# Squared-ReLU attention with a routed feed-forward part: the moving operand of four score chunks laid out in token order by eight transfers

## The chip, the core and the metric

One NeuronCore of one Trainium2 chip runs the whole program as a single launch. The metric is the time of one execution in microseconds of device time; three runs of the kernel before are given by their median. One further execution was taken under the hardware profiler, and every row below comes from that one.

The names used here: PE is TensorE's matmul, PEld its weight load, DVE is VectorE, ACT is ScalarE, POOL is GpSimd, SP is SyncE. An added "q" (SPq, PEldq) means the sequencer of that engine, which issues transfers and waits for semaphores.

## The reference

```python
scores = np.matmul(z, z.transpose(0, 2, 1)) / S      # z: (8, 3136, 64)
attn = np.maximum(scores, 0.0) ** 2
x = u * np.matmul(attn, v)                           # u, v: (8, 3136, 256)
...
s = np.einsum('bsd,d->bs', x, w_gate)                # per batch: the 128 tokens with the largest s
h = np.maximum(x[b, top] @ w1, 0.0)                  # w1: (256, 1024), w2: (1024, 256)
out[b, top] = x[b, top] + sigmoid(s[b, top])[:, None] * (h @ w2)
```

All arithmetic is in float32, and the scores of a batch form a symmetric matrix of 3136 by 3136. The second part, the routed one, is small beside the first and is woven into it. This study is about the first line, `z` times `z` transposed.

## The kernel before, in words

**Chunks and tiles.** The 3136 query tokens of a batch are cut into seven chunks: five of 512 columns (numbers 0 to 4), one of 256 and one of 320. The 3136 keys are cut into tiles of 128 and handled two at a time; such a pair of key tiles for one chunk is a *slot*, and the last half tile is a slot of its own. The program is one list of slots (`slots`), batch after batch and chunk after chunk, and the order of every engine is written out from that list by hand (`tc.manual_schedule()`), with scores issued three slots (`LEAD`) ahead of their use.

**Scores.** `scores` (L413) multiplies, for one slot, the key tiles by the moving operand `Z[b, c]`. A float32 value is carried as a high and a low float32r part; `ZH` and `ZL` hold them, and `Z` stacks the high part on partitions 0 to 63 and the low part on partitions 64 to 127, so that two matmuls for one key tile (one with weights from `ZH`, one with weights from `ZL`) make the full product. A slot of two key tiles thus has four score matmuls in a row, which this text calls a *quartet*: ZH, ZL, ZH, ZL. Then ACT and DVE square the result, split it into `hi` and `lo` (L423, L424, L434, L483), and `mix` (L519) multiplies `V` by it into `acc`, twelve matmuls a slot.

**Symmetry.** Since the scores are symmetric, a square that an earlier chunk computed is not computed again: DVE transposes it in blocks of 32 (L452, L471) into `aT`, SP stores it to HBM (`squares`, L458 and L466) and a later chunk fetches it (`qk`, L362), so that its slot is an *old* one, without score matmuls. A chunk of number c below 5 therefore computes scores only for key tiles from 4c on. Its own second pair of tiles (`is_second`) needs only the last 256 of the 512 columns.

**The layout of z.** The block transposes want the keys of a chunk in a mixed order, so `ZH` and `ZL` hold a chunk of 512 tokens as (t f a): f counts its four groups of 128 tokens, t the four quarters of a group and a the 32 tokens of a quarter. A key tile, 128 neighbouring columns, is then one quarter of each of the four groups. The moving operand has to give its columns in token order, (f t a). `bring_z` (L243 to L266) copies the chunk's columns of `ZH` and `ZL` from SBUF to SBUF into the tile `Z` (two buffers) ahead of the chunk, seven slots before its first one. Two ways of doing it are there:

- a chunk of 512 columns is copied as it lies, by two transfers (L258), one for each half of the partitions, and the matmul then reads it through a view that puts the columns into order, in runs of 32 columns:

```python
Z[b, c] = t.rearrange("p (t f a) -> p f t a", t=GT, a=Q) if w == CH else t
```

- the chunks of 256 and 320 columns are put into order by the transfer itself, 128 columns at a time (L263, and L265 for the last 64 columns): four or six transfers, whose source is gathered in runs of 32 columns (128 bytes); the matmul reads 256 or 320 contiguous columns.

The very first chunk of all is written by ACT and DVE instead of by transfers.

**SP's queue.** Nearly all transfers are issued by SP, in the order in which the program lists them: `z` and `v` of the next batch, the squares stored and fetched, `u`, the results. They rotate through eight semaphores (DMAHW0 to DMAHW7), and an issue waits until the transfer that had its semaphore before it has landed.

Of the kernel before, what the change touches and what calls it, by code (L numbers as in the profile page):

```python
# [19 lines left out]
CH = 512  # L20
GT = 4
Q = 32
# [62 lines left out]
def attention_then_routed_ffn(ctx: ExitStack, tc: tile.TileContext, zt, ut, v, wg, w1, w2, cst, cst16, keys, outs, at, cap):  # L85
# [101 lines left out]
    for o in range(0, W, 2 * D):  # L187
        kk, f = divmod(o, F)
# [11 lines left out]
    def by_rows(z, c0, n):  # L200

        g = c0 // CH * CH
        rows = slice((c0 - g) // P, (c0 - g + n) // P)
        return z[:, g : g + CH].rearrange("p (t f a) -> p f t a", t=GT, a=Q)[:, rows]

    Z = {}
# [38 lines left out]
    def bring_z(b, c):  # L245

        c0, w = CHUNKS[c]
        t = const.tile([P, CH], F32R, name="Z", tag="Z", bufs=2)[:, :w]
        for rows, z in ((slice(0, 64), ZH), (slice(64, P), ZL)):
            if b == 0 and c == 0:  # L250
                src, to = (by_rows(x, 0, CH)[rows] for x in (z, t))
                st = staged["z", 0, 0][rows].rearrange("p (f t a) -> p f t a", t=GT, a=Q)
                if z is ZH:
                    nc.scalar.copy(to, st)
                else:
                    nc.vector.tensor_tensor(to, st, by_rows(ZH, 0, CH)[rows].bitcast(F32), op=ALU.subtract)
            elif w == CH:
                nc.sync.dma_start(t[rows].bitcast(F32), z[rows, c0 : c0 + w].bitcast(F32))  # L258
            else:
                for o in range(0, w, P):  # L260
                    if c0 + o < NJ * P:
                        src = by_rows(z, c0 + o, P)[rows, 0]
                        nc.sync.dma_start(t[rows, o : o + P].rearrange("p (t a) -> p t a", a=Q).bitcast(F32), src.bitcast(F32))  # L263
                    else:
                        nc.sync.dma_start(t[rows, o:].bitcast(F32), z[rows, c0 + o : c0 + w].bitcast(F32))  # L265
        Z[b, c] = t.rearrange("p (t f a) -> p f t a", t=GT, a=Q) if w == CH else t  # L266

    def stage_v(b, g, queues=(nc.sync,) * GT):

# [853 lines left out]
    for b in range(B):  # L1123
        k0 = b * per

        for i in range(NCH):
            if b == 0:
                k = (0, 0, 0, 1, 3, 5, 6)[i]
            elif i < WHOLE:
                k = k0 - per + (i + 1) * SLOTS + 7  # L1130
            else:
                k = k0 - 1 + 4 * (i - WHOLE)
            use = lambda b=b, i=i: prep_z(b, i)
            if b:
                at_slots(k, lambda b=b, i=i: stage_z(b, i), use, 0.6, lead=5 if i < WHOLE else 2)
            elif i > 2:
                at_slot(k, lambda i=i: prep_z(0, i, 1 if i < WHOLE else WHOLE), 0.6, 0.7)
                if i == WHOLE:
                    loads.append((2, lambda: stage_z(0, WHOLE, S + 64 - WHOLE * CH)))
                elif 3 < i < WHOLE:  # L1140
                    loads.append((max(1, k - 3), lambda i=i: more_z(0, i, 1)))
        for g in range(NJ // 2 + 1):
            k = k0 - 10 + 3 * g // 2 if b else max(1, g - 2)
            if b or g > 2:
                at_slot(k, lambda b=b, g=g: prep_v(b, g))
            if (b or g > 4) and g % 2 == 0:
                loads.append((k - (3 if b else 2), lambda b=b, g=g: stage_v(b, g // 2)))
        for c in range(NCH):
            if b or c:
                at_slot(k0 + c * SLOTS - LEAD - 4, lambda b=b, c=c: bring_z(b, c))  # L1150
        for c in range(NCH):
            at_slot(k0 + c * SLOTS + 7, lambda b=b, c=c: load_u(b, c))
# [73 lines left out]
    def start():  # L1226
        warm(12)
        stage_z(0, 0)
        first = moe.tile([P, 1], F32, name="g", tag="g", bufs=2)
        nc.scalar.copy(first, idle[0][:, :1])  # L1230
        stage_z(0, 1, (WHOLE - 1) * CH, CH)
        stage_v(0, 0, (nc.scalar, nc.scalar, nc.sync, nc.sync))
        stage_v(0, 1)
        more_z(0, 2, 1)
        more_z(0, 3, 1)
        low_parts = []
        prep_z(0, 0, on=lambda *x, **how: low_parts.append(lambda: nc.vector.tensor_tensor(*x, **how)))
        bring_z(0, 0)
        for fn in low_parts:
            fn()  # L1240
        prep_z(0, 1)
        more_scores(0)
        prep_v(0, 0, nc.vector)
        busy["pool"] = 3.0
        more_scores(1)
        square_scores()
        prep_v(0, 1)
        settle_scores()
        prep_z(0, 2, 1)
        prep_v(0, 2)  # L1250
        warm(2)
        stage_v(0, 2)

    order = ExitStack()
# [131 lines left out]
```

## Time and profile before

| | |
|---|---|
| median of 3 runs | 2118.13 us (2117.64 to 2118.53) |
| the profiled execution | 2115.92 us |
| its span, first to last instruction | 2114.1 us |
| PE busy | 2095.5 us, 99% |
| DVE, POOL, ACT busy | 1520.9, 1345.6, 1221.6 us |
| DMA queue of SP | 430752 packets, 417.89 MB, 72.2% of 16 engines' span |
| transfers under 512 bytes a packet | 148864 packets |
| score matmuls, L413 | 760 with ZH and 760 with ZL |
| acc matmuls, L519 | 8064 in two large groups |
| granted TensorE clock | full in all 40 slices |

The profile lists busy time by engine, then the chain of waits (followed back from the last instruction), then groups of instructions by line, then the transfers. The end of a matmul is modelled, and successive ones overlap, so that the duration of a matmul row is longer than its share of PE's time. What a matmul really takes from PE is read from the timeline instead: the distance from its start to the start of the next one. A timeline row gives the start of its first instruction, the time up to the modelled end of its last one, the engine, the line, output and inputs, and how many equal instructions stand in the row.

### The profile page before, as it was taken

The numbers are of one execution on the slowest core, as the hardware profiler recorded it, in microseconds if no ns is written. First come the engines' busy times: TensorE is split into PE (matmuls) and PEld (weight loads), VectorE is DVE, ScalarE is ACT, GpSimd is POOL, SyncE is SP. The second block draws the span as 40 slices with busy tenths as digits, with TensorE's granted clock in tenths as the row PEclk, the third lists the DMA queues.
The fourth block names the chain that finished last, engine by engine and source line by source line (L and its number), as shares of the span: only waits on it lengthen the run. The fifth ranks groups of instructions, "written<-read, shape, count | busy, mean of one in ns | idle before, by whom it ended". The sixth has DMA issues, their size and how long they took to land.

```text
span 2114.1 us, 31795 instructions
## 1 busy us (share of the span) xinstructions
PE 2095.5 (99%) x10583; PEld 1754.7 (83%) x10583; DVE 1520.9 (72%) x2304; ACT 1221.6 (58%) x1493; POOL 1345.6 (64%) x703
## 2 busy tenths in 40 slices
PE   8999999999999999999999999999999999999998
PEld 6788988889888898888988889888897888887788
DVE  8767678765877667776678766786667776787776
ACT  7564576545765457654676546755466554765543
POOL 6676577655866558765576655866567656666643
PEclk9999999999999999999999999999999999999999
DMA  7798766788667876778767777677776776765862
GB/s 199 202 260 224 216 186 180 186 235 219 185 192 190 232 219 190 193 192 224 217 193 199 191 223 216 187 201 194 207 236 177 206 187 177 210 193 162 221 175 93
DMA packets 431973, 422.28 MB, mean 200 GB/s; under 512 B 148864, under 2 KB 340160, under 8 KB 428224
## 3 DMA queue, kind: packets, MB, share of 16 engines
q1 hardware_dynamic: 430752, 417.89, 72.2%
q0 software_dynamic: 768, 2.10, 0.3%
q8 instruction: 83, 1.36, 0.3%
q14 instruction: 82, 0.67, 0.1%
q10 hardware_dynamic: 288, 0.26, 0.0%
HBM read 235.31 MB, written 172.23 MB: 193 GB/s over the span
## 4 chain that ended last, share of the span: by engine, by line
PE 87%; DMA 3%; DVE 2%; issue 2%; ACT 2%; POOL 2%; SPq 1%; POOLq 0%; DVEq 0%; ACTq 0%
PE acc L519 71%; PE sc L413 14%; POOL lo L483 1%; ACT a L423 1%; ACT hi L424 1%; PE h L1037 1%; DVE a L434 1%; DMA qk<-squares_narrow 1%; PE y L1081 1%; DMA qk<-squares 0%; DMA squares<-aT 0%; DVE lo L483 0%; SPq L381 0%; DVE ut L564 0%; SPq L466 0%
## 5 line engine op out<-in xcount | busy, mean ns | idle before, releaser
L519 PE MATMUL acc<-hi,V 128*128 128x512 f32 (+2 forms) x5376 | 1232.9, 367 | 3.0 <-ACT hi L424 0.8
L483 POOL TENSOR_TENSOR lo<-a,hi 128x1024 fp32r<-128x1024 f32 (+2 forms) x327 | 756.2, 2315 | 609.7 <-DVE a L434 484.3
L519 PEld LDWEIGHTS acc<-hi,V 128*128 128x128 f32 x5376 | 932.9, 188 | 171.2 <-DVE ut L564 8.9
L423 ACT ACTIVATE a<-sc 128x1024 f32<-128x1024 f32 (+4 forms) x408 | 363.3, 890 | 540.9 <-PE sc L413 431.2
L519 PE MATMUL acc<-lo,V 128*128 128x512 f32 (+2 forms) x2688 | 668.7, 365 | 3.2 <-POOL lo L483 3.1
L519 PEld LDWEIGHTS acc<-lo,V 128*128 128x128 f32 x2688 | 474.3, 188 | 86.8 <-POOL lo L483 5.6
L434 DVE TENSOR_TENSOR a<-sc,a 128x1024 f32<-128x1024 f32 (+3 forms) x334 | 338.2, 1012 | 278.3 <-ACT hi L424 257.7
L391 ACT CAST hi<-qk 128x1024 fp32r<-128x1024 f32 (+2 forms) x320 | 275.5, 863 | 245.0 <-PE acc L519 201.5
L452 DVE STREAM_TRANSPOSE aT<-a 128x512 f32<-128x512 f32 (+1 forms) x520 | 341.0, 691 | 84.4 <-ACT a L429 57.3
L424 ACT ACTIVATE hi<-a 128x1024 fp32r<-128x1024 f32 (+4 forms) x408 | 377.4, 925 | 18.1 <-PE acc L519 0.5
L483 DVE TENSOR_TENSOR lo<-qk,hi 128x1024 fp32r<-128x1024 f32 (+2 forms) x223 | 299.5, 1350 | 72.1 <-ACT hi L391 69.6
L413 PE MATMUL sc<-Z,ZH 128*128 128x512 f32 (+2 forms) x760 | 282.0, 375 | 3.4 <-DVE a L434 2.4
L413 PE MATMUL sc<-Z,ZL 128*128 128x512 f32 (+2 forms) x760 | 281.9, 375 | 0.7 <-DVE ZL L120 0.7
L483 POOL TENSOR_TENSOR lo<-qk,hi 128x1024 fp32r<-128x1024 f32 (+2 forms) x97 | 188.8, 1950 | 57.7 <-ACT hi L391 39.1
L413 PEld LDWEIGHTS sc<-Z,ZH 128*128 128x128 f32 x760 | 142.8, 188 | 34.5 <-DVE a L434 6.1
L413 PEld LDWEIGHTS sc<-Z,ZL 128*128 128x128 f32 x760 | 142.7, 188 | 26.4 <-DVE ZL L120 1.1
L120 POOL TENSOR_TENSOR V<-vst,V 128x512 fp32r<-128x512 f32 x89 | 126.4, 1424 | 31.5 <-ACT V L119 27.0
L585 POOL TENSOR_TENSOR ut<-x,w_run 128x1024 f32<-128x1024 f32 (+2 forms) x52 | 127.3, 2449 | 24.4 <-DVE x L576 22.4
L429 ACT ACTIVATE a<-a 128x1024 f32<-128x1024 f32 x74 | 78.5, 1061 | 2.3
L119 ACT CAST V<-vst 128x512 fp32r<-128x512 f32 x95 | 57.8, 608 | 38.3 <-DMA vst<-in_v 38.1
L120 POOL TENSOR_TENSOR ZL<-zst,ZH 128x512 fp32r<-128x512 f32 (+2 forms) x56 | 76.0, 1362 | 2.9 <-ACT ZH L119 2.8
L564 DVE SCALAR_TENSOR_TENSOR ut<-acc,ut 128x512 f32<-128x512 f32 (+2 forms) x112 | 64.0, 612 | 17.7 <-PE acc L519 17.4
(151 smaller groups left out, 1038.7 us busy)
## 6 DMA issues: line engine op xcount, KB each, us to landing
squares<-aT SPq DMA_DIRECT2D x160, 512.0 KB, 3.5
qk<-squares SPq DMA_DIRECT2D x320, 256.0 KB, 5.7
squares_narrow<-aT SPq DMA_DIRECT2D x320, 128.0 KB, 4.1
qk<-squares_narrow SPq DMA_DIRECT2D x80, 512.0 KB, 5.3
vst<-in_v SPq DMA_DIRECT2D x190, 128.0 KB, 3.5
out<-x SPq DMA_DIRECT2D x162, 128.0 KB, 3.3
ut<-in_ut SPq DMA_DIRECT2D x40, 512.0 KB, 5.1
squares_own<-aT SPq DMA_DIRECT2D x39, 256.0 KB, 2.1
```

The source lines that it names most:

```text
L120: (lo_on or nc.vector.tensor_tensor)(lo, src, hi.bitcast(F32), op=ALU.subtract)
L391: nc.scalar.copy(by(hi), src)
L413: nc.tensor.matmul(ps[:, q], z[:, j * P : (j + 1) * P], mov, start=z is ZH, stop=z is ZL)
L423: nc.scalar.activation(a, ps[:, :n], AF.Relu)
L424: nc.scalar.activation(pieces[0][0](hi), pieces[0][1], AF.Square)
L429: nc.scalar.activation(a, a, AF.Square)
L434: square = lambda: nc.vector.tensor_tensor(a[rows], ps[rows, :n], a[rows], op=ALU.mult)
L452: nc.vector.transpose(to, a[rows, q].rearrange("p (m t a) -> p m t a", t=GT, a=Q))
L483: on.tensor_tensor(view(lo), src, view(hi).bitcast(F32), op=ALU.subtract)
L519: nc.tensor.matmul(ac[h], w, mov, start=first and h not in started, stop=stop)
L564: nc.vector.scalar_tensor_tensor(xT[:, h, :w], acc[b, c][h], SCALE * SCALE, xT[:, h, :w], op0=ALU.mult, op1=ALU.mult)
L585: nc.gpsimd.tensor_tensor(wx, runs, consts["wg_run"].rearrange("p (o r) -> p o r", o=1).broadcast_to([P, NB, RUN]), op=ALU.mult,)
```

## The change

In the batches 1 to 7 (the first one is left as it is), the chunks 1 to 4 (the first chunk of a batch is left as it is) take the second way: 128 columns at a time, four transfers from `ZH` and four from `ZL`, and `Z` is then in the order (f t a). The view through which the matmuls read it becomes "p (f t a) -> p f t a", which is contiguous. Nothing else is changed; the 28 chunks (7 batches of 4) have eight transfers in place of two.

```diff
@@ bring_z
-            elif w == CH:
+            elif (b == 0 or c == 0) and w == CH:
                 nc.sync.dma_start(t[rows].bitcast(F32), z[rows, c0 : c0 + w].bitcast(F32))
             else:
                 for o in range(0, w, P):
...
                         nc.sync.dma_start(t[rows, o : o + P].rearrange("p (t a) -> p t a", a=Q).bitcast(F32), src.bitcast(F32))
...
-        Z[b, c] = t.rearrange("p (t f a) -> p f t a", t=GT, a=Q) if w == CH else t
+        order = "p (t f a) -> p f t a" if (b == 0 or c == 0) and w == CH else "p (f t a) -> p f t a"
+        Z[b, c] = t.rearrange(order, t=GT, a=Q) if w == CH else t
```

The added line moves the numbers of all lines behind it up by one: L413, L458, L466 and L519 are L414, L459, L467 and L520 in the changed kernel.

The queue of SP at chunk 1 of batch 2, before (64x512 and 64x4x32 are the shapes written; the brackets name the semaphores that the issue waits for):

```order
555 L258 DMA Z<-ZH 64x512 [waits DMAHW7_49,PE_49]
556 L258 DMA Z<-ZL 64x512 [waits DMAHW0_49]
557 L458 DMA squares_0_92<-aT 512x1x256 [waits DMAHW1_49,DVE_49]
558 L554 DMA ut<-in_ut 128x2x512 [waits DMAHW2_49,DVE_49]
559 L466 DMA squares_narrow_0_93<-aT 32x4x256 [waits DMAHW3_49,DVE_49]
```

The same place in the changed kernel:

```order
579 L263 DMA Z<-ZH 64x4x32 [waits DMAHW7_49,PE_49]
580 L263 DMA Z<-ZH 64x4x32 [waits DMAHW0_49]
581 L263 DMA Z<-ZH 64x4x32 [waits DMAHW1_49]
582 L263 DMA Z<-ZH 64x4x32 [waits DMAHW2_49]
583 L263 DMA Z<-ZL 64x4x32 [waits DMAHW3_49]
584 L263 DMA Z<-ZL 64x4x32 [waits DMAHW4_49]
585 L263 DMA Z<-ZL 64x4x32 [waits DMAHW5_49]
586 L263 DMA Z<-ZL 64x4x32 [waits DMAHW6_49]
587 L459 DMA squares_0_92<-aT 512x1x256 [waits DMAHW7_49,DVE_49]
588 L555 DMA ut<-in_ut 128x2x512 [waits DMAHW0_49,DVE_49]
589 L467 DMA squares_narrow_0_93<-aT 32x4x256 [waits DMAHW1_49,DVE_49]
```

Six issues more stand ahead of the stores and fetches that follow, and the eight take all eight semaphores once round.

PE at the first quartet of the same chunk, before:

```order
1390 L519 MATMUL acc<-hi,V 128x512 x7
1391 L413 MATMUL sc<-Z,ZH 128x512 [waits DMAHW0_49,DMAHW7_49,DVE_49,PE_49]
1392 L413 MATMUL sc<-Z,ZL 128x512
1393 L413 MATMUL sc<-Z,ZH 128x512
1394 L413 MATMUL sc<-Z,ZL 128x512
```

In the changed kernel:

```order
1390 L520 MATMUL acc<-hi,V 128x512 x7
1391 L414 MATMUL sc<-Z,ZH 128x512 [waits DMAHW3_49,DMAHW4_49,DMAHW2_49,DMAHW5_49,DMAHW1_49,DMAHW6_49,DMAHW0_49,DMAHW7_49,DVE_49,PE_49]
1392 L414 MATMUL sc<-Z,ZL 128x512
1393 L414 MATMUL sc<-Z,ZH 128x512
1394 L414 MATMUL sc<-Z,ZL 128x512
```

PE's instructions and their order are the same; the first score matmul of the chunk waits for eight transfers in place of two.

## Rows read from the trace of the kernel before

**Rows 1.** The page, part 1: busy time, share of the span and instructions by engine.

```profile
PE 2095.5 (99%) x10583; PEld 1754.7 (83%) x10583; DVE 1520.9 (72%) x2304; ACT 1221.6 (58%) x1493; POOL 1345.6 (64%) x703
```

**Rows 2.** Chunks 1-4, batch 2: length; busy PE, PEld, DVE, ACT, POOL; clock; DMA share.

```profile
568.60:738.00 169.40, 169.32 (x777) 137.19 (x776) 124.20 (x191) 93.82 (x102) 106.93 (x48) 1.00 0.74 200
```

**Rows 3.** Timeline of PE, first two quartets of chunk 1 of batch 2.

```profile
568.68 0.40 PE L413 MATMUL sc<-Z,ZH 128*128 128x512 f32 x1
...
569.62 1.09 PE L519 MATMUL acc<-lo,V 128*128 128x512 f32 x4
570.55 1.08 PE L519 MATMUL acc<-hi,V 128*128 128x512 f32 x4
571.46 0.40 PE L413 MATMUL sc<-Z,ZH 128*128 128x512 f32 x1
...
572.40 1.09 PE L519 MATMUL acc<-hi,V 128*128 128x512 f32 x4
573.33 0.85 PE L519 MATMUL acc<-lo,V 128*128 128x512 f32 x3
```

**Rows 4.** Timeline of PE, old slots in chunk 4, then its quartet of 256 columns.

```profile
708.01 1.99 PE L519 MATMUL acc<-hi,V 128*128 128x512 f32 x8
...
715.27 0.28 PE L413 MATMUL sc<-Z,ZH 128*128 128x256 f32 x1
...
715.74 1.07 PE L519 MATMUL acc<-lo,V 128*128 128x512 f32 x4
716.65 0.62 PE L519 MATMUL acc<-hi,V 128*128 128x512 f32 x2
```

**Rows 5.** Timeline of PE, first quartets of the chunks of 256 and 320 columns.

```profile
738.77 0.28 PE L413 MATMUL sc<-Z,ZH 128*128 128x256 f32 x1
...
739.25 0.28 PE L519 MATMUL acc<-hi,V 128*128 128x256 f32 x1
...
761.60 0.31 PE L413 MATMUL sc<-Z,ZH 128*128 128x320 f32 x1
...
762.18 0.31 PE L519 MATMUL acc<-hi,V 128*128 128x320 f32 x1
```

**Rows 6.** Timeline of SP's queue around the two transfers of chunk 1.

```profile
557.63 0.58 SPq L258 DMA_DIRECT2D Z<-ZH  x1
558.26 1.03 SPq L258 DMA_DIRECT2D Z<-ZL  x1
559.45 0.56 SPq L458 DMA_DIRECT2D squares<-aT  x1
560.15 0.55 SPq L554 DMA_DIRECT2D ut<-in_ut  x1
562.62 2.16 SPq L466 DMA_DIRECT2D squares_narrow<-aT  x4
...
568.64 4.08 SPq L466 DMA_DIRECT2D squares_narrow<-aT  x6
```

**Rows 7.** Timeline of SP's queue: the four transfers of the 256-column chunk.

```profile
719.12 1.34 SPq L263 DMA_DIRECT2D Z<-ZH  x2
720.51 1.32 SPq L263 DMA_DIRECT2D Z<-ZL  x2
```

**Rows 8.** By line, L258 and then L263: time from issue to landing.

```profile
DMA to landing us min/median/max: 2.2/3.3/6.1
...
DMA to landing us min/median/max: 1.9/2.7/7.9
```

**Rows 9.** By line, L413: its waits on PE's sequencer, ns min/median/max.

```profile
L413 PEldq EVENT_SEMAPHORE  x129: 51/51/2782, 6.5 to 2061.2; - x129
```

**Rows 10.** Chunk 4: issue of the fetch behind z, its use, and the page's landing.

```profile
684.21 2.57 SPq L362 DMA_DIRECT2D qk<-squares  x4
...
695.28 1.05 ACT L391 CAST hi<-qk 128x1024 fp32r<-128x1024 f32 x1 [1.36 <-PE acc L519]
...
qk<-squares SPq DMA_DIRECT2D x320, 256.0 KB, 5.7
```

## The prediction

> **What bounds the kernel now.** I read the busy times first. PE is busy for 2095.5 us, 99% of the span; no other engine that computes is above 72% [rows 1]. [...] So time can be won here only if matmuls follow each other at a shorter distance, and is lost only where PE is made to wait. [...]
>
> Next I read the timeline of PE, as distances from start to start. In a long run of acc matmuls of 512 columns (old slots in chunk 4) the row of eight at 708.01 is followed by such rows of 4, 8, 4 and 8 up to 715.27: 32 matmuls in 7.26 us, 0.2269 us each [rows 4]. That is the pace of PE when nothing is in its way. A quartet of score matmuls with 512 columns takes longer: from 568.68 to 569.62 it is 0.94 us for four, 0.235 each [rows 3]. The acc matmuls right behind it are slower too: 0.93 us for the four from 569.62 on, 0.2325 each, though they read contiguous `lo`; the next four, from 570.55 to 571.46, are back at 0.2275 [rows 3]. The second quartet, from 571.46, repeats this: 0.94 and then 0.93 [rows 3]. Score quartets that read contiguous columns show no such excess: the one of the 256-column chunk takes 0.48 us, and the one of the 320-column chunk 0.58 us, 0.12 and 0.145 each [rows 5].
>
> **The change part by part.**
>
> *What PE gains.* Two things of the slow quartets go away together with their cause, if the cause is that the moving operand is read in 16 runs of 32 columns. The stretch from 568.68 to 573.33 holds two quartets and twelve acc matmuls, 20 in all, in 4.65 us [rows 3]. At the undisturbed pace they would take 20 x 0.2269 = 4.538 us, so that a quartet with what follows it costs 0.112 / 2 = 0.056 us too much. Of this 0.94 - 4 x 0.2269 = 0.0325 us lies in the four score matmuls themselves and 0.0235 us behind them. How many quartets: chunk c has (24 - 4c) / 2 pairs of key tiles, of which one is the 256-column pair, so 9, 7, 5 and 3 for chunks 1 to 4, 24 a batch and 168 in seven batches. The half tile at the end of each chunk adds two score matmuls of 512 columns, 56 in all. The whole excess is 168 x 0.056 = 9.4 us and 56 x 0.008 = 0.5 us, together **9.9 us**; of this 168 x 0.0325 + 0.5 = 6.0 us is in the score matmuls alone. The 112 score matmuls of the 256-column pairs gain nothing: today, in runs of 32, they take 0.47 us a quartet, from 715.27 to 715.74 [rows 4], no more than the contiguous ones [rows 5].
>
> That last sentence is also the strongest thing against the gain. If every run of 32 columns had a price, eight runs would show half the excess of sixteen, and they show none. I still take the 9.9 us, since quartets of the same four instructions differ in width and in runs only: 256 in runs has no excess, 256 and 320 without runs have none, and 512 in runs is the only kind with one. A price that is hidden up to a certain length fits this as well as one for the width alone does. The other end of this term is 0.
>
> [...]
>
> *What SP pays.* The two transfers take SP from 557.63 to 559.29, 1.66 us [rows 6]. Four transfers of the new kind take from 719.12 to 721.83, 2.71 us [rows 7], so eight take about 5.4 us: 3.8 us more in each of 28 chunks, 106 us of SP's time. It is hidden as far as SP waits anyway: behind the two transfers SP issues the store at 559.45 and `u` at 560.15, and is done with these at 560.70, but issues the next store only at 562.62, 1.9 us later, because DVE is not ready; the narrow stores are issued until 564.78, a fetch of four behind them takes 2.57 us at most (the length of another one, [rows 10]), until 567.35, and SP goes on only at 568.64, 1.3 us later [rows 6]. So the store at 559.45 and `u` come 3.8 us late, the narrow stores and the fetch some 1.9 us, and from 568.64 on at most 0.6 us is left. The worst place is chunk 4, where the fetch of an old square stands right behind z: it is issued until 686.78, would be issued until 690.6, and with 5.7 us to land is there at 696.3, for an ACT instruction that starts at 695.28 today [rows 10]. ACT is up to 1.0 us late there, seven times, 7 us at most; but its output is for a slot that PE reaches later, since scores and squares are made three slots ahead, and one old slot is 12 matmuls of 0.2269, 2.7 us. I take 0 of it, with 7 us as the upper end.
>
> *What PE waits for.* The first score matmul of a chunk gets six waits more. A wait for a semaphore that is met costs PE's sequencer 51 ns, the least and the median [rows 9]; six of them are 0.31 us a chunk and 8.6 us over 28, if PE stood still for all of it. It does not need to: the longest such wait lasts 2782 ns [rows 9], while PE is idle for 0.08 us in all in the stretch of four chunks [rows 2], so that the sequencer must run well ahead of PE. The lower end is 0, and I take **1 us** for this and the late ACT together.
>
> *When z is there.* Today the second transfer is issued by 559.29 and the first quartet starts at 568.68, a lead of 9.4 us [rows 3, 6]. It shrinks to 5.6 us, and a landing of 2.7 us, the median of the new kind [rows 8], leaves 2.9 us. No wait is taken.
>
> *DMA engines.* The bytes stay the same, cut into sixteen times as many source pieces of 128 bytes. The transfers of this kind land after 2.7 us, the larger ones of the old kind after 3.3 us [rows 8]; I cost it at nothing, with the rival below as the other end.
>
> **The sum.** 9.9 - 1.0 = 8.9 us less: 2115.92 - 8.9 = 2107.0 us for the profiled execution. That execution is 2.2 us below the median of the runs, 2118.13, so for a median I predict 2118.13 - 8.9 = **2109.2 us**.
>
> **The rivals.**
>
> *Half the gain.* The score matmuls become faster, but the slow acc matmuls behind them stay, because any change from one kind of matmul to the other disturbs the pace. For it: they read contiguous data and are slow all the same [rows 3]. Against it: behind the 256-column quartet, which is the same change of kind, four acc matmuls take 0.91 us, from 715.74 to 716.65, as in a long run [rows 4]. Time: 2118.13 - 6.0 + 1.0 = 2113.1 us.
>
> *No gain.* The excess belongs to the width of 512 or to where a quartet stands, and the runs are read for free. For it: eight runs cost nothing today [rows 4]. Against it: acc matmuls are 512 wide too and keep 0.2269 us [rows 4]. Time: 2118.13 + 1.0 = 2119.1 us. [...]
>
> *z comes too late.* The place is the first quartet of chunk 1, whose lead shrinks to 5.6 us. One of the transfers of the new kind took 7.9 us to land [rows 8]. If the last of the eight always took that long, PE would stand for 7.9 - 5.6 = 2.3 us at chunk 1 of seven batches, 16.1 us; with the gain of 9.9 the time is 2118.13 + 16.1 - 9.9 = 2124.3 us, slower. It eats up the whole gain once the landing there is over 5.6 + 9.9 / 7 = 7.0 us. At chunk 4, whose z is issued before 684.21, ACT uses the fetch behind it only at 695.28 [rows 10], so that its lead is longer. For it: eight transfers in a row share the DMA engines, which are 74% busy there [rows 2]. Against it: the median is 2.7 us. [...]
>
> That the change does not do what it says I leave without a chance: the new view is contiguous, and PE's order is the same.
>
> **How the numbers follow.** Full gain 0.52, half the gain 0.16, no gain 0.21, late z 0.11. A measurement of this kernel can tell about 0.2%, 4.2 us, from no change, so faster begins below 2113.9 us. Full gain is faster. Half the gain, at 2113.1, lies on the border: 0.10 of it counts as faster and 0.06 as the same. Of no gain 0.19 is the same and 0.02 slower (where a bound of the waits, 7 or 8.6 us, is met). Late z is slower with 0.10 and the same with 0.01. That gives 0.62 faster, 0.26 the same and 0.12 slower. The range: with no cost, and with the starts read 0.01 us off in 4.65 (0.8 us over 168 quartets), the full gain ends at 2107.4; the spread of the runs, 0.9 us, takes it to 2106.5. Above, it takes in half the gain and no gain at 2119.1 with half of that spread, 2119.6. Outside lie late z and the costlier waits, under 2 in 10. For the likeliest case alone the range is 2106.5 to 2112.
>
> **What would show it.** In the profile after: quartets of 512 columns in chunks 1 to 4 at 0.91 us in place of 0.94, the four acc matmuls behind them at 0.91 in place of 0.93, and the quartets of chunk 0 of every batch, which are not changed, still at 0.94; half the gain would show the first without the second, and no gain neither. On SP eight issues of about 0.67 us; the first quartet of chunk 1 some 3 us behind the last landing, and PE without idle time ahead of it. The prediction is wrong if the changed quartets keep 0.94 us, or if PE shows a wait for Z, or for ACT in chunk 4.

## The result, and the profile after

The changed kernel takes 2147.3 us (median of 4 runs, 2146.44 to 2148.2) beside 2118.33 us for the kernel before in the same session (4 runs, 2117.64 to 2119.84): ratio 1.0142, 95% interval 1.0129 to 1.0154. It is 29 us slower; 8.9 us less had been predicted. The profiled execution took 2148.2 us (span 2146.4).

The page of the changed kernel, parts 1 and 4: busy time by engine, and the chain that ended last.

```profile
PE 2102.2 (98%) x10583; PEld 1758.6 (82%) x10583; DVE 1529.2 (71%) x2304; ACT 1221.3 (57%) x1493; POOL 1341.0 (62%) x703
PE 71%; DMA 10%; DVE 6%; ACT 3%; issue 3%; SPq 3%; POOL 3%; POOLq 0%; DVEq 0%; ACTq 0%
```

PE still has 98%, hardly less than before [rows 1], but 32.3 us of span lie between the two, and the chain now runs through transfers for 10% of its length (3% before).

The stretches of chunks 1 to 4 of batch 2 in the changed kernel, each from its first score matmul to the next one's: length; busy PE, PEld, DVE, ACT, POOL; clock; DMA share; GB/s.

```profile
575.10:620.10 45.00, 43.75 (x195) 35.50 (x194) 35.34 (x67) 28.65 (x30) 29.19 (x14) 1.00 0.64 176
620.10:666.30 46.20, 44.48 (x199) 35.70 (x198) 33.49 (x63) 25.39 (x27) 29.01 (x14) 1.00 0.72 188
666.30:706.60 40.30, 40.30 (x199) 32.66 (x198) 29.64 (x31) 20.84 (x23) 25.75 (x11) 1.00 0.75 179
706.60:748.10 41.50, 41.41 (x194) 33.91 (x193) 28.20 (x32) 19.55 (x24) 20.95 (x10) 1.00 0.91 257
```

Before, PE was idle for 0.08 us in all four together [rows 2]. Now it is idle for 1.25 us in chunk 1 and 1.72 us in chunk 2, and for 0.09 us at most in chunks 3 and 4. So in this batch the loss has a place: two stalls, one in each of chunks 1 and 2.

PE's timeline in chunk 1 of batch 2 of the changed kernel (it answers to [rows 3]), then its first stall.

```profile
575.13 0.39 PE L414 MATMUL sc<-Z,ZH 128*128 128x512 f32 x1
...
576.05 1.07 PE L520 MATMUL acc<-lo,V 128*128 128x512 f32 x4
576.96 1.07 PE L520 MATMUL acc<-hi,V 128*128 128x512 f32 x4
577.86 0.39 PE L414 MATMUL sc<-Z,ZH 128*128 128x512 f32 x1
...
578.79 1.07 PE L520 MATMUL acc<-hi,V 128*128 128x512 f32 x4
579.69 1.07 PE L520 MATMUL acc<-lo,V 128*128 128x512 f32 x4
...
583.70 0.40 PE L414 MATMUL sc<-Z,ZL 128*128 128x512 f32 x1
585.34 1.21 PE L520 MATMUL acc<-hi,V 128*128 128x512 f32 x4 [1.25 <-DVE ut L565]
```

The gain is there: the quartet takes 576.05 - 575.13 = 0.92 us (0.94 before), the four `lo` behind it 0.91 (0.93), the second quartet 0.93 (0.94) and its four 0.90 (0.93); the 20 matmuls from 575.13 to 579.69 take 4.56 us in place of 4.65. Then, 8.8 us into the chunk, PE waits for DVE's L565, the reading of the finished chunk's `acc`, whose bank the next `acc` needs.

SP's timeline ahead of that stall in the changed kernel (it answers to [rows 6]):

```profile
563.12 3.01 SPq L263 DMA_DIRECT2D Z<-ZH  x4
566.17 2.60 SPq L263 DMA_DIRECT2D Z<-ZL  x4
568.87 0.56 SPq L459 DMA_DIRECT2D squares<-aT  x1
569.52 0.57 SPq L555 DMA_DIRECT2D ut<-in_ut  x1
570.19 2.51 SPq L467 DMA_DIRECT2D squares_narrow<-aT  x4
572.75 2.13 SPq L363 DMA_DIRECT2D qk<-squares  x4
575.14 4.78 SPq L467 DMA_DIRECT2D squares_narrow<-aT  x6
```

The two DVE instructions that decide, before and in the changed kernel: the transposes of the chunk's own square, and the reading of `acc`.

```profile
574.36 0.77 DVE L471 STREAM_TRANSPOSE aT<-a 128x256 f32<-128x256 f32 x2 [1.06 <-DMA squares_narrow<-aT]
576.17 1.27 DVE L564 SCALAR_TENSOR_TENSOR ut<-acc,ut 128x512 f32<-128x512 f32 x2
```

```profile
582.81 0.77 DVE L472 STREAM_TRANSPOSE aT<-a 128x256 f32<-128x256 f32 x2 [3.08 <-DMA squares_narrow<-aT]
584.62 1.27 DVE L565 SCALAR_TENSOR_TENSOR ut<-acc,ut 128x512 f32<-128x512 f32 x2
```

Counted from the first quartet (568.68 before, 575.13 after), the second set of narrow stores starts at the same time, -0.04 and 0.01 us. But the fourth store of that row is issued at 1.27 us before and at 2.05 us after: the second issue takes 1.04 us where it took 0.43. The transfer that had its semaphore, the second of the first four narrow stores, was issued 4.3 us ahead of it (571.17 to 575.49) in place of 6.0 (562.99 to 568.99), so that the likely reason is that it has not landed: these stores land 4.6 us after their issue by the median in this kernel, 3.4 us before. And from the fourth issue to L471/L472 it is 4.41 us before and 5.63 after: the fourth store lands later, 5.5 us from its issue in place of 4.3. The fetch is now issued right ahead of these stores, which may be why; no run takes that apart for chunk 1. So the transposes, which need the `aT` buffer that these stores empty, start at 5.68 us before and 7.68 us after, and L564/L565 at 7.49 and 9.49. This chain had no 2 us to give: before, the first of the two L564 had ended at 8.16 us and PE started the matmul that needs it at 8.91, so 0.75 us were to spare, and the other 1.25 us are PE's stall.

Chunk 2 of the same batch in the changed kernel: SP, then DVE, POOL and PE.

```profile
613.83 1.88 SPq L363 DMA_DIRECT2D qk<-squares  x4
615.81 4.27 SPq L467 DMA_DIRECT2D squares_narrow<-aT  x5
...
624.10 0.71 DVE L453 STREAM_TRANSPOSE aT<-a 64x512 f32<-64x512 f32 x1 [3.15 <-DMA squares_narrow<-aT]
627.00 2.36 POOL L484 TENSOR_TENSOR lo<-a,hi 128x1024 fp32r<-128x1024 f32 x1 [6.60 <-DVE a L435]
629.41 0.73 PE L520 MATMUL acc<-lo,V 128*128 128x512 f32 x2 [1.72 <-POOL lo L484]
```

The same buffers, another user: here the half tile's transpose waits for the first four narrow stores, then DVE's square L435, POOL's `lo` and PE are late. Counted from the first quartet (612.44 before, 620.11 here), these stores are issued from -4.3 us on in place of -7.9: SP has little idle time ahead of them here, and 3.6 us of the burst reach them.

The waits of the whole program, by line waiting and what ended the wait: us in all, times, longest. The kernel before, then the changed one.

```profile
DVE aT L471 <- DMA squares_narrow<-aT: 10.7, 7, 2.6
DVE aT L452 <- DMA squares_narrow<-aT: 2.5, 2, 2.0
PEld acc L519 <- DVE ut L564: 8.9, 19, 0.8
PE acc L519 <- DVE ut L564: 0.8, 3, 0.4
PE acc L519 <- POOL lo L483: 3.1, 3, 1.9
PE xeT L1011 <- DMA xe<-out,ids: 1.3, 1, 1.3
```

```profile
DVE aT L472 <- DMA squares_narrow<-aT: 37.9, 15, 4.7
DVE aT L453 <- DMA squares_narrow<-aT: 19.4, 8, 3.2
PEld acc L520 <- DVE ut L565: 25.8, 25, 3.4
PE acc L520 <- DVE ut L565: 15.2, 9, 3.0
PE acc L520 <- POOL lo L484: 10.2, 9, 1.8
PE xeT L1012 <- DMA xe<-out,ids: 4.0, 1, 4.0
```

Of the seven waits in the row of L471, six, 8.2 us together, stand in chunk 1 of batches 1 to 6; the seventh is in batch 0.

Both kernels have the same 10583 PE instructions in the same order, so that each distance from start to start can be compared with its own of before. Over the 28 changed chunks, the differences below 30 ns add up to -5.6 us (this is the pace), and the larger ones to +35.1 us (the stalls, with the half-speed matmuls of the last section among them): 19.6 in chunk 1, 13.3 in chunk 2 (some 4 of them in batch 7, at the wait for `xe` of the routed part and behind it; why `xe` comes later was not looked into), 2.2 in chunks 3 and 4. Together 29.5 of the 32.3 us between the spans. The experiments are read in the same two columns below.

### The profile page after: what moved, and what is told of

It reads as the page before. It is cut to its first block, busy times and chain, and to the rows that moved or that the text cites. A ratio compares the mean times of both kernels' runs of the same rounds, so it can differ in the third digit from the quotient of the medians.

```text
span 2146.4 us, 32046 instructions
## 1 busy us (share of the span) xinstructions
PE 2102.2 (98%) x10583; PEld 1758.6 (82%) x10583; DVE 1529.2 (71%) x2304; ACT 1221.3 (57%) x1493; POOL 1341.0 (62%) x703
## 2 busy tenths in 40 slices
DMA packets 488423, 422.32 MB, mean 197 GB/s; under 512 B 208896, under 2 KB 400192, under 8 KB 484672
## 4 chain that ended last, share of the span: by engine, by line
PE 71%; DMA 10%; DVE 6%; ACT 3%; issue 3%; SPq 3%; POOL 3%; POOLq 0%; DVEq 0%; ACTq 0%
PE acc L520 59%; PE sc L414 10%; DMA squares_narrow<-aT 5%; POOL lo L484 2%; DVE a L435 2%; ACT a L424 2%; DMA ut<-in_ut 2%; ACT hi L425 1%; DMA vst<-in_v 1%; DVE aT L453 1%; DMA qk<-squares_narrow 1%; SPq L263 1%; PE h L1038 1%; DMA qk<-squares 1%; DVE lo L484 1%
## 5 line engine op out<-in xcount | busy, mean ns | idle before, releaser
L520 PE MATMUL acc<-hi,V 128*128 128x512 f32 (+2 forms) x5376 | 1237.9, 368 | 18.3 <-DVE ut L565 15.2
L520 PEld LDWEIGHTS acc<-hi,V 128*128 128x128 f32 x5376 | 936.1, 189 | 189.1 <-DVE ut L565 25.8
L520 PE MATMUL acc<-lo,V 128*128 128x512 f32 (+2 forms) x2688 | 670.2, 366 | 10.6 <-POOL lo L484 10.2
L424 ACT ACTIVATE a<-sc 128x1024 f32<-128x1024 f32 (+4 forms) x408 | 363.4, 891 | 530.4 <-PE sc L414 420.2
L520 PEld LDWEIGHTS acc<-lo,V 128*128 128x128 f32 x2688 | 474.1, 188 | 95.9 <-POOL lo L484 16.2
L435 DVE TENSOR_TENSOR a<-sc,a 128x1024 f32<-128x1024 f32 (+3 forms) x334 | 338.2, 1012 | 251.5 <-ACT hi L425 230.9
L453 DVE STREAM_TRANSPOSE aT<-a 128x512 f32<-128x512 f32 (+1 forms) x520 | 341.0, 691 | 87.3 <-ACT a L430 45.3
L484 DVE TENSOR_TENSOR lo<-qk,hi 128x1024 fp32r<-128x1024 f32 (+2 forms) x223 | 303.9, 1371 | 88.9 <-ACT hi L392 87.6
L414 PE MATMUL sc<-Z,ZH 128*128 128x512 f32 (+2 forms) x760 | 280.9, 374 | 3.2 <-DVE a L435 2.4
L414 PE MATMUL sc<-Z,ZL 128*128 128x512 f32 (+2 forms) x760 | 279.6, 372 | 0.7 <-DVE ZL L120 0.7
L484 POOL TENSOR_TENSOR lo<-qk,hi 128x1024 fp32r<-128x1024 f32 (+2 forms) x97 | 187.9, 1940 | 59.3 <-ACT hi L392 32.3
L414 PEld LDWEIGHTS sc<-Z,ZH 128*128 128x128 f32 x760 | 142.8, 188 | 33.2 <-DVE a L435 6.1
L414 PEld LDWEIGHTS sc<-Z,ZL 128*128 128x128 f32 x760 | 142.6, 188 | 26.1 <-DVE ZL L120 1.1
L565 DVE SCALAR_TENSOR_TENSOR ut<-acc,ut 128x512 f32<-128x512 f32 (+2 forms) x112 | 64.0, 612 | 17.8 <-PE acc L520 17.5
```

The costliest lines, as they stand in the source:

```text
L414: nc.tensor.matmul(ps[:, q], z[:, j * P : (j + 1) * P], mov, start=z is ZH, stop=z is ZL)
L424: nc.scalar.activation(a, ps[:, :n], AF.Relu)
L435: square = lambda: nc.vector.tensor_tensor(a[rows], ps[rows, :n], a[rows], op=ALU.mult)
L453: nc.vector.transpose(to, a[rows, q].rearrange("p (m t a) -> p m t a", t=GT, a=Q))
L484: on.tensor_tensor(view(lo), src, view(hi).bitcast(F32), op=ALU.subtract)
L520: nc.tensor.matmul(ac[h], w, mov, start=first and h not in started, stop=stop)
```

## The experiments

Theory A: the eight issues in a row hold SP, narrow stores land late, their `aT` buffer comes free late, and DVE, POOL and PE follow. Rivals: B, the 128-byte pieces load the DMA engines; C, the contiguous read itself.

**1. Eight transfers, old order.** The kernel before, in the 28 chunks:

```diff
...
             elif w == CH:
-                nc.sync.dma_start(t[rows].bitcast(F32), z[rows, c0 : c0 + w].bitcast(F32))
+                for o in range(0, w, P):
+                    nc.sync.dma_start(t[rows, o : o + P].bitcast(F32), z[rows, c0 + o : c0 + o + P].bitcast(F32))
```

> This kernel is the one before with its two transfers of 64x512 cut into eight of 64x128 (512 bytes a piece), in the 28 changed chunks; the matmuls read Z in runs of 32 as before. Theory A (the burst on SP): eight issues in a row hold SP for 5.6 us in place of 1.6, stores and fetches behind them come late, and PE pays for that at chunks 1 and 2. Then this kernel is as slow as the changed one and lacks its gain of 2 to 3 us in the matmuls: 2147 to 2152 us, with PE waiting some 15 us for L565 and 10 us for L484 as in the changed kernel. Theory B (the pieces): 128-byte pieces slow the DMA engines for the stores and fetches beside them. Then 512-byte pieces cost nothing: 2117 to 2121 us. Theory C (the read): contiguous moving columns change PE's pace or the clock: also 2117 to 2121 us.

Measured 2146.91 us, before 2116.94: ratio 1.0144 (1.0128 to 1.0159). Its waits (L474, L522 and L567 are L472, L520 and L565 of the changed kernel):

```profile
DVE aT L474 <- DMA squares_narrow<-aT: 35.8, 15, 4.4
PE acc L522 <- DVE ut L567: 12.4, 8, 2.6
```

The whole loss in time without the new order and without 128-byte pieces. B and C can't be its main cause.

**2. The same eight, spread.** Two transfers a slot, at slots 10, 9, 8 and 7 ahead.

```diff
...
-                at_slot(k0 + c * SLOTS - LEAD - 4, lambda b=b, c=c: bring_z(b, c))
+                for i in range(GT) if b and 1 <= c < WHOLE else (None,):
+                    at_slot(k0 + c * SLOTS - LEAD - (4 if i is None else 7 - i), lambda b=b, c=c, i=i: bring_z(b, c, i))
```

> The changed kernel with the same eight transfers, but issued as pairs (ZH and ZL of one group of 128 columns) at slots 10, 9, 8 and 7 ahead of the chunk, in place of all eight at 7. SP works as long in all, never more than 1.4 us for z in one piece. Theory A (the burst on SP): the stores and fetches are hardly late, and what is left is the gain of the matmuls, by the changed kernel's chunks 3 and 4 some 0.1 us a chunk, 2 to 3 us: 2114 to 2120 us. Theory A2 (not the burst but SP's total time or the turn of the eight semaphores): 2130 to 2147 us. Theory B (128-byte pieces slow the DMA engines): the pieces are the same, 2140 to 2148 us. Theory C (the read itself): 2147 us.

Measured 2116.41, before 2116.94: 0.9999 (0.999 to 1.0008). The same transfers without the burst: the loss is gone, so it was not SP's total time.

**3. From GpSimd.**

```diff
-                        nc.sync.dma_start(
+                        (nc.gpsimd if b and 1 <= c < WHOLE else nc.sync).dma_start(
...
```

> The changed kernel with its eight transfers issued by GpSimd, through semaphores of their own, at the same slot; SP issues even two transfers a chunk less than before. Theory A (the burst on SP): no store and no fetch is late, 2114 to 2118 us if GpSimd has the time for eight issues beside its lo (it is busy for 64% before); if an issue there holds it for as long as one holds SP, 5.6 us, lo comes late at one or two slots of each chunk and PE waits for L484, up to 28 x 3 = 84 us more. Theory B (128-byte pieces): 2147 us, with waits for stores as in the changed kernel. Theory C (the read): 2147 us without them.

Measured 2154.97, before 2116.94: 1.0188 (1.0174 to 1.0202). One group of issues, PE's largest wait, and DVE's wait for narrow stores:

```profile
L263 POOL DMA_DIRECT2D Z<-ZH x112 | 69.7, 633 | 0.0
PE acc L520 <- POOL lo L484: 19.3, 27, 2.1
DVE aT L472 <- DMA squares_narrow<-aT: 2.0, 1, 2.0
```

GpSimd is held for 0.633 us an issue, as SP is in the changed kernel (0.632 us the median with `ZH`), and its own `lo` comes late instead. The price moved with the issues: without the burst on SP the wait of L472 is 2.0 us in place of 37.9, and PE's for L565 0.3 in place of 15.2. The page of this run counts 151552 packets under 512 bytes, that of the changed kernel 208896, so that it says nothing on the pieces of 128 bytes.

**4. From ScalarE.**

```diff
-                        nc.sync.dma_start(
+                        (nc.scalar if b and 1 <= c < WHOLE else nc.sync).dma_start(
...
```

> The changed kernel with its eight transfers issued by ScalarE at the same slot. SP is free of them, but they share the eight semaphores with SP's transfers. Theory A (the burst on SP): SP's stores and fetches are in time, and ScalarE, busy for 58% before, is held for about 5 us at seven slots ahead of each chunk, with scores made three slots ahead: between 2115 us (hidden) and 2118 + 28 x 2.5 = 2188 us. Theory A2 (the turn of the semaphores, not SP's time): PE waits for L565 and L484 as in the changed kernel, about 2147 us. Theory B (pieces): 2147 us.

Measured 2179.89, before 2116.94: 1.0296 (1.028 to 1.0312), inside A's range, which is too wide to decide anything; ScalarE stands for 106.9 us ahead of its L424, 24 times, until transfers of z have landed, and PE waits 24.4 us for L435, by the profile its largest wait. ScalarE's sequencer has 2% of the chain that ended last, at L263, in place of 0% before. The rest of the 63 us was not taken apart.

**5. Own buffer for the own transposes.** The changed kernel, with L472 off the `aT` rotation; the room comes from a throw-away output of the routed part, which moves to another tile.

```diff
-            t = work.tile([P, GT, 2, P], F32, name="aT", tag="aT", bufs=2).rearrange("p m q x -> p (m q x)")[:, :CH]
+            t = work.tile([P, CH], F32, name="aT", tag="aTown", bufs=1)
...
```

> The changed kernel with one link of the assumed chain taken out: the transposes of a chunk's own square (L472) write to a tile of their own (2 KB a partition, one buffer; the room comes from a throw-away output of the routed part, which moves to another tile) in place of the two aT buffers, so that they need not wait for the narrow stores to land. Theory A, with this link: DVE no longer waits for squares_narrow at L472 (37.9 us in the changed kernel, 10.7 before), L565 is in time at chunk 1, PE's 15.2 us for L565 go, and chunk 1 costs 2 to 5 us over seven batches in place of 17; chunk 2, where L453 waits for its buffer, keeps its 11 us: 2129 to 2138 us. Theory A3 (the burst hurts by late u or late fetched squares, and the store's buffer is beside the path): 2143 to 2148 us.

Measured 2131.14, before 2117.31: 1.0073 (1.0054 to 1.0092). DVE in chunks 1 and 2 of batch 2:

```profile
578.12 0.77 DVE L472 STREAM_TRANSPOSE aT<-a 128x256 f32<-128x256 f32 x2
...
621.27 0.71 DVE L453 STREAM_TRANSPOSE aT<-a 64x512 f32<-64x512 f32 x1 [3.61 <-DMA squares_narrow<-aT]
```

With the burst still there, L472 no longer waits, and chunk 1's stalls fall from 19.6 to 0.5 us. Late `u` or late squares (A3) would have kept them. Chunk 2 has the other user and keeps its loss.

**6. Chunks 3 and 4 alone.** The same in the line that sets `order`.

```diff
-            elif (b == 0 or c == 0) and w == CH:
+            elif (b == 0 or c < 3) and w == CH:
```

> The changed kernel with the eight transfers in chunks 3 and 4 alone, 14 in place of 28; chunks 1 and 2 are as before. Theory A (the burst hurts where narrow stores stand behind it, chunks 1 and 2): chunks 3 and 4 cost nothing and gain in the matmuls, by the changed kernel's distances of PE some 0.2 us a chunk 3 and 0.1 us a chunk 4, 2.5 us in all: 0 to 3 us less than the kernel before of the same chip. The rival (each burst costs the same, 29 us over 28): half of it, 14.5 us more.

Measured 2118.51, before 2117.31: 1.0005 (0.9996 to 1.0014). Not half the loss: there is no price that every burst pays, since in chunks 3 and 4 it costs nothing that can be seen. Nor is there a gain; PE's pace gives 1.8 us, and one longer wait takes 2.4 us back (the routed part's `xe` in batch 7, 3.7 us in place of 1.3).

**7. Spread, old order.** The second experiment's slots, the first one's transfers.

> The spread of the second experiment (pairs at slots 10, 9, 8 and 7 ahead), but with pieces of 64x128 as they lie, so that the matmuls read Z in runs of 32 as before. It differs from the spread kernel in the read of z (and in the source pieces of 512 in place of 128 bytes) alone. If the shorter distances that PE shows with contiguous columns (some 6 us over the 28 chunks) are a gain in time, this kernel is 4 to 8 us slower than the spread one: 2120 to 2125 us. If they are given back elsewhere, it is the same within 2 us.

Measured 2120.14, before 2117.31: 1.0017 (1.0008 to 1.0026), against 0.9999 with the new order. The difference, 0.0018 or 3.8 us, is a little under the range expected: the read of contiguous columns is worth time. The two intervals together leave some 1 to 6.5 us, so that this is not told apart from the 5.9 us that PE's pace shows. The two kernels also differ in their source pieces, 512 bytes here and 128 there; a price of the smaller ones would work against this gain.

**8. One transfer a slot, chunk 0 too.** As 2, but one transfer a slot, in every chunk of batches 1 to 7.

```diff
...
-            elif (b == 0 or c == 0) and w == CH:
+            elif b == 0 and w == CH:
...
-                at_slot(k0 + c * SLOTS - LEAD - 4, lambda b=b, c=c: bring_z(b, c))
+                n = 2 * -(-CHUNKS[c][1] // P)
+                for i in range(n) if b else (None,):
+                    at_slot(k0 + c * SLOTS - LEAD - (4 if i is None else 3 + n - i), lambda b=b, c=c, i=i: bring_z(b, c, i))
```

> Token order for all chunks of the batches 1 to 7, chunk 0 among them, and one transfer a slot: eight (or four, six for the last two chunks) in the slots up to the seventh ahead of the chunk. SP is held by z for some 0.7 us a slot. Theory A: no store is late by more than that, the 28 chunks gain some 6 us and chunk 0, with 77 quartets more at 0.037 us, some 3 us: 2108 to 2113 us. The rival (each of the eight semaphores comes round more often, and any added issue costs something): 2115 to 2125 us.

Measured 2113.09, before 2117.31: 0.9981 (0.9972 to 0.999), just above the range expected, with 4.2 us of the 9 hoped for. Faster than both kernels; chunk 0's share of it was not measured apart.

**9. Fetch behind the narrow stores.** Kernel 5, with one fetch of chunk 2 a slot later.

```diff
-        at_slot(k, lambda key=(b, c, g): fetch(*key))
+        at_slot(k + (1 if b and c == 2 and g == 0 else 0), lambda key=(b, c, g): fetch(*key))
```

> The kernel of the fifth experiment (changed kernel, own transposes in a tile of their own; 2131 us, its loss of 14.5 us now all in chunk 2), with the fetch of the first old square of chunk 2 (four issues) one slot later, so that on SP the first four narrow stores stand between u and the fetch in place of behind it. Theory A for chunk 2 (the burst, u and the fetch hold back the first four narrow stores, DVE's transpose of the half tile at L453 waits for their landing, then L435, L484 and PE): the stores are issued some 2 us sooner, L453 waits at most 1 us in place of 2.6 to 3.6, and chunk 2 gives back 8 to 14 us: 2117 to 2123 us. The rival (the fetched square is what comes late, for ACT at L392): the fetch is later still, and the time is 2131 to 2140 us.

Measured 2117.62, before 2116.35: 1.0002 (0.9993 to 1.0011). SP and DVE at chunk 2 of batch 2:

```profile
603.28 2.59 SPq L263 DMA_DIRECT2D Z<-ZL  x4
606.28 0.40 SPq L555 DMA_DIRECT2D ut<-in_ut  x1
606.79 1.86 SPq L467 DMA_DIRECT2D squares_narrow<-aT  x4
608.70 2.19 SPq L363 DMA_DIRECT2D qk<-squares  x4
...
613.22 0.70 DVE L453 STREAM_TRANSPOSE aT<-a 64x512 f32<-64x512 f32 x1
```

The first four narrow stores go ahead of the fetch, L453 has no wait here, and 1.0073 becomes 1.0002, some 15 us, with the burst unchanged. What is left in chunk 2 is the wait for `xe` in batch 7 (3.8 us, 1.3 before) and what follows it. It is the order of stores and fetch behind the burst, not the late fetch, that cost chunk 2 its time.

**10. One per slot with the own buffer.** The diffs of 8 and 5 together.

> The one-per-slot kernel of the eighth experiment (0.9981 of the kernel before) with the own transposes in a tile of their own. If L472 still costs PE something there (DVE waits 9.0 us for narrow stores at L472 in that kernel), it is 1 to 4 us faster than without: 2109 to 2112 us, 0.996 to 0.998 of before. If that wait is off PE's path, it is the same, 0.998.

Measured 2111.97, before 2116.35: 0.9978 (0.9969 to 0.9987). Not told apart from 0.9981. The fastest median ratio of all.

**11. The kernel before with the own buffer.** The diff of 5 alone.

> The kernel before, with the own transposes in a tile of their own and nothing else. DVE waits 10.7 us at L472 there, and PE 0.8 us for L565 behind it: 0 to 2 us faster than before at the most, 2115 to 2118 us. A larger gain would mean that the fifth experiment's gain was only partly that of the changed kernel's late stores.

Measured 2115.74, before 2116.35: 0.9997 (0.9988 to 1.0006). The buffer is worth nothing measurable without the burst, so what it gave in 5 was the burst's loss.

**12. Pieces of 128 bytes, old order.** The kernel before, in the 28 chunks:

```diff
...
+                for f in range(GT):
+                    src, to = (by_rows(x, o, CH)[rows, f] for x, o in ((z, c0), (t, 0)))
+                    nc.sync.dma_start(to.bitcast(F32), src.bitcast(F32))
```

> The kernel of the first experiment (eight transfers, z as it lies) with another cut: each of the eight takes 64x4x32, in pieces of 128 bytes as in the changed kernel, and writes them where they lay, so that the matmuls read runs of 32 as before. It is the changed kernel without its new order. If the pieces of 128 bytes cost nothing, it is as slow as the first experiment, 1.0144 of before, and the changed kernel's 1.0142 lacks a gain of some 5.6 us in PE's distances. If the pieces cost what the new order gains, the price is seen here: 1.0142 + 0.0027 = 1.017 of before, some 2152 to 2153 us.

Measured 2151.28, before 2116.63: 1.0171 (1.0151 to 1.0191). As A with a price for the pieces expects; but the interval touches that of 1 (up to 1.0159), so that a price of the pieces, some 5 us by the middles, is likely and not settled. The pieces also lie apart in `Z` here, 128 bytes each, where the four of a transfer of the changed kernel lie in a row of 512, so that the price need not be the changed kernel's; the pages of both count the same 208896 packets under 512 bytes.

PE's distances against the kernel before in the 28 chunks, us, one profiled execution each:

| kernel | ratio | pace (under 30 ns) | stalls, chunk 1 | chunk 2 | 3 and 4 |
|---|---|---|---|---|---|
| changed | 1.0142 | -5.6 | 19.6 | 13.3 | 2.2 |
| 1 eight, old order | 1.0144 | 0.1 | 16.2 | 10.0 | 0.1 |
| 12 pieces, old order | 1.0171 | 0.0 | 21.2 | 8.9 | 1.0 |
| 5 own buffer | 1.0073 | -5.8 | 0.5 | 16.9 | 1.5 |
| 9 and fetch behind | 1.0002 | -6.2 | -0.2 | 5.2 | 1.3 |
| 2 spread | 0.9999 | -5.9 | 3.5 | 1.8 | 0.5 |
| 7 spread, old order | 1.0017 | -0.1 | 1.3 | 1.2 | 0.0 |
| 8 one per slot | 0.9981 | -5.6 | 0.1 | 0.8 | 0.5 |
| 10 and own buffer | 0.9978 | -5.8 | -0.2 | 0.1 | 0.3 |

## Why the prediction was wrong

**The step that failed** is "What SP pays", with its sentence "It is hidden as far as SP waits anyway" and its end, "from 568.64 on at most 0.6 us is left". The issue times came out as worked out there: eight issues in 5.65 us (5.4 predicted), and the second narrow stores start on time to 0.05 us. But SP's idle time was taken for the slack of what SP issues. What counts is the landing, and who waits for it: DVE's transposes need the buffer that the store empties. One row of the waits of before shows that this landing already ended last: L471 waited for it 10.7 us, six times out of seven in chunk 1. Behind it PE had little to spare: in chunk 1 of batches 1 to 6 it started the matmul that needs `acc` 0.05 to 0.8 us after the first L564 had ended (1.6 us in batch 7, which has no stall there). The 19 waits of PE's weight loads for L564 are no second sign of it, since 18 of them stand elsewhere, and with the own buffer in the kernel before (experiment 11) they still come to 9.0 us. The prediction followed SP to its next wait, and then the fetch to ACT, and never asked who waits for the stores. It also read chunk 1 and chunk 4 alone; in chunk 2 the first narrow stores are issued 3.6 us late. It took 0 for all this, with 7 us for ACT in chunk 4 as the upper end; experiment 1 measures the burst at 30 us.

**The rotation of the eight semaphores** was described and left out of the price. In both kernels the second set of narrow stores takes the semaphores of the first set, eight issues earlier; with SP without a pause between, it comes round to them sooner, and issues are longer: 0.8 us of the 2.0 us in chunk 1 of batch 2. SP's rows show a store issue of 1.04 us in place of 0.43 where the transfer before it on the semaphore is 4.3 us old in place of 6.0.

**What PE gains** was right in kind, and too large: 5.6 us of 9.9. Both halves are there, so "half the gain", which kept the slow acc matmuls, is wrong as a mechanism, and "no gain" too. The size came from 20 matmuls of chunk 1 with the undisturbed pace of 0.2269 as its end; the quartets reach 0.92 and 0.93 us, not 0.91, and over 168 quartets it is 5.6 / 168 = 0.033 us each in place of 0.056. The medians say where it is missing: the four matmuls behind a quartet go from 0.925 to 0.906 us, nearly as predicted, but the quartet itself only from 0.939 to 0.922. The quartets of chunk 0, which are not changed, stay at 0.940. In time it is 3.8 us by experiments 2 and 7, with some 1 to 6.5 us possible. So the runs of 32 columns (128 bytes) are not read for free in quartets of 512: these went from 0.94 to 0.92 us with contiguous columns, and experiments 2 and 7 show it in the time (0.9999 against 1.0017).

**PE's waits, z's landing, chunk 4.** Ten waits on the first score matmul cost nothing that can be seen (experiment 10 has 0.2 us of stalls in all in the 28 chunks). The last z transfer was issued by 568.77, 6.4 us ahead of the quartet, and PE never waited for it: the rival "z comes too late" got the sign right with the wrong place. ACT in chunk 4, feared at 7 us, can be at most the 1.7 us of stalls there; PE's rows name DVE's L565 for them (1.1 us in batch 1, 0.6 in batch 7). **DMA engines at nothing**: likely short, by some 5 us if experiment 12 against 1 is taken for it, not settled.

## What to carry to other kernels

Idle time of a queue is not the slack of what it carries: before putting more issues on a queue, list who waits for the landing of each transfer behind them, buffers that a store empties among them, and look in the waits of before for rows in which that wait already ends last. A burst of issues can cost what the same issues spread over slots don't (1.0142 against 0.9999 here, 0.9981 with one a slot and chunk 0 changed too). A queue on another engine is no way out if that engine is held for each issue (0.633 us on GpSimd) and has others waiting for its own work (1.0188 from GpSimd, 1.0296 from ScalarE).

## What was unexpected of the hardware

After four of its longer waits PE went on at a granted clock of 0.50. PE's timeline at chunk 1 of batch 1 of the changed kernel, and the windows behind two such waits (the columns as above, the clock third from the end):

```profile
317.54 0.39 PE L414 MATMUL sc<-Z,ZL 128*128 128x512 f32 x1
320.25 1.29 PE L520 MATMUL acc<-hi,V 128*128 128x512 f32 x4 [2.32 <-DVE ut L565]
321.34 1.05 PE L520 MATMUL acc<-lo,V 128*128 128x512 f32 x2
322.19 2.33 PE L520 MATMUL acc<-hi,V 128*128 128x512 f32 x5
...
319.90:323.10 3.20, 2.85 (x9) 2.23 (x10) 3.03 (x11) 1.43 (x2) 3.20 (x2) 0.70 0.05 17
1378.20:1381.40 3.20, 3.20 (x11) 2.49 (x11) 3.03 (x11) 2.10 (x2) 3.20 (x2) 0.68 0.01 3
```

From 321.34 to 322.19 two matmuls take 0.85 us, 0.427 each where 0.227 is the pace. The granted clock is 0.50 from 321.34 to 322.19 and 1.00 from 320.30 to 321.00; seven or eight matmuls take that long, about 1.4 us more in all. This follows the waits at chunk 1 of batches 1, 5 and 6 and the 3.98 us for `xe` in batch 7, some 5.6 us of the stalls in all; in batch 2, after 1.25 us, the clock stays at 1.00 in the window above. It does not follow every long wait: at chunk 1 PE's distance is 3.36 us in batch 3 and 2.65 in batch 4, against 2.60 to 2.71 in batches 1, 5 and 6, and the next ones are at full pace.
